# A tile of its own for one set of weight sums, and a new order of adds around two round entries, in a TensorE-bound retention and ELU kernel

## The chip, the cores and the metric

The kernel runs on one core of a Trainium2 chip. The metric is the time of one execution on the device in microseconds (us); lower is better. The kernel computes in float32 (the weights come as float64 bits and are converted at the start).

## The reference, cut to what matters

```
# q, k, v: (4, 8, 768, 64); w_in: (512, 2048); w_out: (2048, 512)
for t in range(S):
    state = gamma * state + einsum('bhd,bhe->bhde', k[:, :, t], v[:, :, t])
    y[:, :, t] = scale * einsum('bhd,bhde->bhe', q[:, :, t], state)
x = y.transpose(0, 2, 1, 3).reshape(3072, 512)
h = x @ w_in
g = where(h > 0, h, exp(minimum(h, 0)) - 1)       # ELU
out = g @ w_out
```

A retention layer with eight heads gives 3072 tokens of 512 values; two matrix products with an ELU between them follow.

## The kernel before, in words

**Tokens.** The 3072 tokens come as six groups of 512 (four chunks of 128 each). Group 0 is multiplied plainly, group 1 with one or two levels of a seven-product scheme, and groups 2 to 5 in two *rounds* of 1024 tokens (`nb` = 0 and 1) with two levels. The retention of a group (`scores`, `states`, `outputs`, cut into `retention_step`s) is laid between the products of an earlier stage. A chunk of q, k and v (1 MB) is loaded into one of four rotating buffers of the pool `ldpool`, tag `chunk` (`load`, L113), and POOL scales its v (`scale_v`, L293).

**The seven products.** A product of 2x2 blocks is made of seven block products instead of eight: inputs are combined by four subtractions beforehand (`quarters_of`, L892), weights by four sums S1 to S4, and the results are put together by adds. The outer products are called M1 to M7 (`j` in the code), the inner ones 1 to 7 (`k`). The results of the outer level are the four blocks C11, C12, C21 and C22.

**The first matrix in a round.** M2, M3, M1 and M7 are made of inner products in eight *steps* (`ORDER1`, `at` = 0 to 7, two halves of each: M2 in steps 0 and 1, M3 in 2 and 3, M1 in 4 and 5, M7 in 6 and 7). `big_twice` (matmuls at L1150) emits a step in pieces: product 1; products 2, 6, 7; product 5; product 4; product 3. ACT lifts results out of PSUM (L1161), DVE adds the others (`plus(r, t)`, L1165: `plus(0,0)` after product 2, `plus(1,1)` after 5, `plus(1,0)` after 4). The loop interleaves two steps, so that PE runs: product 1 of a step, 4 of the step before, 2, 6, 7 of this one, 3 of the one before, 5 of this one. PSUM has a bank `b` and a bank `d`, and two banks `a`. Product 7 of a step uses bank `d`, which `plus(1,0)` of the step before frees.

M1 is kept in two chunk buffers (`held_x`). M2 lands in C11's place, and `big_c11(r, at)` (L1218, one 128x1024 add) adds M1 to a quarter of it. M6, M4 and M5 are not kept: in the *tile loop* (n = 0 to 7, a tile of 128 features each) they are accumulated by `rest(m, j)` (L1197) onto a PSUM bank that ACT filled with M1's tile (`seed`, L1650) and, for M4, onto bank `d`, filled with what the first bank then holds (`second_seed`, L1654, on DVE for odd m and on ACT for even m). `sum_` (L1206) adds the kept results to C21, C12 and C22. The inputs of M6, M5 and M4 are three 128x1024 subtractions of `big_layer_x` (L1118) at the end of its generator: `t1` in step 6, `t2` in step 7 and `t4` behind the steps. An ELU of a tile has two ACTIVATEs on ACT (`begin`, L1212 and L1213, into one of three buffers `r`) and one DVE instruction (`end`, L1214).

**The second matrix** (`second_big`, matmuls at L1246) starts with four quarter inputs of C11 (`input_parts`, L892, 128x1024 each), which the tile loop advances by `next(sec)`.

**Sums of weights in round 0.** For M2, M3, M1 and M7, `combine_small(j)` makes S1 to S4 (four 128x512 DVE instructions, L850), and six stores send them to a scratch in DRAM (`send_small`, L664; for M7 by `sent(7)` in step 3). From there the weights come back piece by piece (L830) into a ring of eight buffers `wq`: `done` gives a buffer free and fetches the next piece on the list, and pieces of M1 and M7 are `blocked` until they are sent. M1's and M7's sums use the same tile, the one of C22 (`gq["C22"]`, shown as gC in the profile). Other stores (`stores`) send the plain weights of M2, M3, M1, M7 and of the layers for round 1.

**What sets the order.** The schedule is by hand: every engine runs its instructions in the order in which the code emits them, and waits for semaphores where data or a buffer isn't ready. All DMAs are issued by SP in one queue. `some(steps, n)`, `run(steps)` and `next(...)` advance the generators; `small_at` and `parts_of` say which step emits what of the weights' sums and of the inputs.

Of the kernel before, what the change touches and what calls it, by code (L numbers as in the profile page):

```python
# [10 lines left out]
FP32 = mybir.dt.float32  # L11
# [8 lines left out]
def kernel(  # L20
# [33 lines left out]
    nc = tc.nc  # L54
    PSUM = bass.MemoryType.PSUM
    P = nc.NUM_PARTITIONS
# [19 lines left out]
    ldpool = ctx.enter_context(tc.tile_pool(name="ldpool", bufs=4))  # L76
# [247 lines left out]
    def scores(tb, pp):  # L324

        sc = [ps_r.tile([P, 2, HP, D], FP32, name="sc", tag="r") for _ in range(2)]
        for x in range(2):
            score_products(sc, tb, pp, x)
        for a in range(2):
            nc.vector.tensor_tensor(  # L330
                out=raw[tb * CPB + 2 * pp + a][0][:, 1].rearrange("p h c -> p (h c)").rearrange("p (n t) -> p n t", t=D),
                in0=sc[a].rearrange("p x h t -> p (x h) t"),
                in1=cmask.unsqueeze(1).to_broadcast([P, 2 * HP, D]), op=ALU.mult,
            )
# [371 lines left out]
    def bank(x):  # L706
        return ps_f.tile([P, 2, TH], FP32, name="p" + x, tag=x, bufs=2 if x == "a" else 1)
# [133 lines left out]

    def combine_small(j):

        if j in (1, 7):
            t = gq["C22"].rearrange("p a t -> p (a t)").rearrange("p (k m c) -> p k m c", k=4, m=4)
        else:
            t = stage.tile([P, 4, 4, P], FP32, name="wi", tag="stage")
        a11, a12, a21, a22 = (W_IN[j][:, 2 * r : 2 * r + 2, :, c, :] for r in range(2) for c in range(2))
        s1, s2, s3, s4 = (t[:, k].rearrange("p (n f) c -> p n f c", f=2) for k in range(4))
        tt = lambda o, x, y, op: nc.vector.tensor_tensor(out=o, in0=x, in1=y, op=op)  # L850
        tt(s1, a21, a22, ALU.add)
        yield
        tt(s2, s1, a11, ALU.subtract)
        yield
        tt(s3, a11, a21, ALU.subtract)
        yield
        tt(s4, a12, s2, ALU.subtract)
        for at in range(2):
            to = scratch3[AMONG[j], at]
            mine = t[:, :, 2 * at : 2 * at + 2].rearrange("p k f d -> p k (f d)")  # L860
            to_send.append((to[1].rearrange("p (k c) -> p k c", k=2), mine[:, 1:3]))
            to_send.append((to[2][:, 0:256], mine[:, 0]))
            to_send.append((to[3][:, 0:256], mine[:, 3]))
# [239 lines left out]
    def big_x(j):  # L1103

        x, t, first_k = xb2 if j == 3 else xa, next_ts(), 0 if j == 1 else 2
        yield from inner_x(j, t, *(x[:, first_k + k, TH * u : TH * u + TH] for k in range(2) for u in range(2)))
# [97 lines left out]
    def big_sum(x, m, ps):  # L1204

        nc.vector.tensor_tensor(out=tile_of(x, m), in0=ps, in1=tile_of("C22" if x == "C21" else x, m), op=ALU.add)  # L1206
# [9 lines left out]
    def big_c11(r, at):  # L1216
        g = G["C11"][r][:, at]
        nc.vector.tensor_tensor(out=g, in0=g, in1=G["M1"][r][:, at], op=ALU.add)  # L1218
# [234 lines left out]
    def run(steps):  # L1453
        for _ in steps:
            pass
# [8 lines left out]
    def some(steps, count):  # L1464
        for _ in itertools.islice(steps, count):
            pass
# [75 lines left out]
    def retention_step(tb, step):  # L1542
        if step == 0:
            scores(tb, 0)
            scores(tb, 1)
        elif step == 1:
            states(tb, 0)
            states(tb, 1)
        else:
            outputs_step(tb, step - 2)  # L1550
# [57 lines left out]
    sec = second_twice(1, lambda: run(big_x(2)))  # L1608
# [11 lines left out]
    for s in sec:  # L1620
        if s == "first":
            step += 1
        at = (step, s if s in ("first", "middle") else "end")
# [16 lines left out]
    for nb in range(NB):  # L1640
        more = nb + 1 < NB
        qa, qd, ends = {}, {}, {}
# [8 lines left out]

        def second_seed(m):
            qd[m] = bank("d")
            (nc.vector.tensor_copy if m % 2 else nc.scalar.copy)(qd[m], qa[m])  # L1654

        def sum_(x, m):
            big_sum(x, m, qd[m] if x == "C21" else qa[m])

        def begin(x, *ms):
            for m in ms:  # L1660
                ends[x, m] = big_elu(x, m)

        def end(x, *ms):
            for m in ms:
                ends.pop((x, m))()
# [5 lines left out]
        def sent(j):  # L1671
            send_small()
            blocked.discard((2, "t", j))
            fetch()
# [9 lines left out]
        def side(at, place):  # L1684
            if nb == 0 and at in small_at and small_at[at][place]:
                j, n = small_at[at][place]
                some(smalls[j], n)
                if n == 3:
                    sent(j)
            if at in parts_of:  # L1690
                some(xparts, parts_of[at][place])
# [6 lines left out]
        for at, (j, sub) in enumerate(ORDER1):  # L1698
            if at == 4:
                held_x = [ldpool.tile([P, 2048], FP32, name="chunk", tag="chunk") for _ in range(2)]  # L1700
                G["M1"] = [x.rearrange("p (n f t c) -> p n f t c", n=2, f=2, t=2) for x in held_x]
            cur = big_twice(nb, j, sub)
            next(cur)
            if at in (6, 7):
                begin("C11", {6: 0, 7: 4}[at])
            if at:
                next(tail, None)
            else:
                run(tail)
            if at in (6, 7):  # L1710
                big_c11(1, at - 6)
            if at == 7:
                end("C11", 0, 1)
            side(at, 0)
            if at == 1 and nb == 0:
                retention_step(3, 2)
            next(cur)
            side(at, 1)
            if nb == 0:
                if at == 0:  # L1720
                    scores(3, 1)
                elif at == 1:
                    retention_step(3, 3)
            run(tail)
            if at == 7:
                seed(0)
            next(cur)
            tail = cur
            if at in (5, 6):
                big_c11(0, at - 5)  # L1730
            if at in (6, 7):
                begin("C11", {6: 1, 7: 5}[at])
            if at == 7:
                end("C11", 4)
            if nb == 0:
                if at == 0:
                    retention_step(3, 1)
                elif at == 1:
                    retention_step(3, 4)
                    run(tail)  # L1740
            side(at, 2)
            if nb == 0:
                if at in (4, 5):
                    bring(groups[0], at - 4)
                stores[at]()
                send_small()
        sec = second_big(nb, (lambda: run(big_x(2))) if more else lambda: None)
        LAST = 2 * NQ - 1
        next(tail)
        rest(0, 6)  # L1750
        second_seed(0)
        some(xparts, 1)
        run(tail)
        seed(1)
# [2 lines left out]
        for n in range(2 * NQ):  # L1757

            if n == 0:
                rest(0, 4)  # L1760
                sum_("C21", 0)
            if n < LAST:
                rest(n + 1, 6)
            if n == LAST - 1 and nb == 0:
                ts_slots[2:2] = [
                    w_all[:, 2 * k : 2 * k + 2, 3072:3584].rearrange("p n (f t) -> p n f t", f=2) for k in range(2)
                ]
            if n:
                begin("C12", n - 1)
            late = {1: 6, 3: 7}.get(n)  # L1770
            if late:
                end("C11", late)
            if n + 2 <= LAST:
                seed(n + 2)
            if n:
                begin("C22", n - 1)
                end("C21", n - 1)
                end("C12", n - 1)
            else:
                begin("C11", 3)  # L1780
                end("C11", 2)
            if n:
                rest(n, 4)
                sum_("C21", n)
            if n < LAST:
                second_seed(n + 1)
            begin("C21", n)
            if n:
                end("C22", n - 1)
            else:  # L1790
                end("C11", 3)
            if n in (0, 2):
                begin("C11", 6 + n // 2)
            if more and n in (1, 5):
                bring(groups[0], 2 + n // 4)
            if n >= LAST - 1:
                next(sec)
                next(sec)
            rest(n, 5)
            sum_("C12", n)  # L1800
            sum_("C22", n)
        next(sec)
        begin("C12", LAST)
        next(sec)
# [10 lines left out]
        for s in sec:  # L1815
# [3 lines left out]
            at = (step, s if s in ("first", "middle") else "end")  # L1819
            if more and at in VISITS:  # L1820
                n = VISITS.index(at)
# [60 lines left out]
```

## Time and profile before

| | |
|---|---|
| runs | 631.17, 630.06, 629.51 us; median 630.06 |
| profiled execution | 631.84 us, of which the span from first to last instruction is 630.0; mean granted TensorE clock 0.991 |
| instructions | 13421 |
| L1150 | x4 (one product of a step): 1.03 us, the next one starts 0.86 to 0.87 later |
| L1197 | x4: 1.88 us, the next one starts 1.72 later |
| L1165, L1206, L1214, L850 (128x512 on DVE) | 0.68 us, the next one starts 0.60 later |
| L1218, L1118, L892 in `second_big` (128x1024 on DVE) | 1.21 to 1.22 us |
| L1161, L1650, L1654 on ACT | 0.57 to 0.59 us |
| DMA | 125.13 MB, mean 199 GB/s |

Of the span, round 0's eight steps take from about 239 to 303 us and its tile loop to 346 us; its second matrix follows, and then round 1 in the same form, with its tile loop from 501 to 541 us. The profile divides the span into 40 slices of 15.75 us; a digit is the busy share of a slice in tenths. An "idle" time stands with the releaser, the instruction or DMA whose end ended the wait; where several semaphores are waited for, the last one by the profile is named.

### The profile page before, as it was taken

What the parts mean: (1) busy time and instruction counts of PE and PEld (TensorE: products, weight loads), DVE (VectorE), ACT (ScalarE), POOL (GpSimd) and SP (SyncE); (2) the same over time, 40 slices, a digit from 0 to 9 for tenths busy, and PEclk for the clock granted to TensorE, in tenths of its full rate; (3) what the DMA queues carried; (4) which work ended last, traced back from release to release, by engine and by line L of the source; (5) the groups of instructions that cost most, each with busy time, mean ns of one, the idle gap of its engine ahead of it and who ended that gap; (6) DMA issues with size and microseconds to landing.
All of it is one profiled execution on the core that took longest, in us unless ns stands there. A gap on an engine that the chain in (4) does not pass through costs nothing.

```text
span 630.0 us, 13421 instructions
## 1 busy us (share of the span) xinstructions
PE 615.2 (98%) x5446; PEld 482.9 (77%) x5446; DVE 498.0 (79%) x778; ACT 259.8 (41%) x444; POOL 25.5 (4%) x30
## 2 busy tenths in 40 slices
PE   7999999999999999979999999999999999999997
PEld 5764568888888998868544888888888744688886
DVE  5769789989788885557888987898546888888885
ACT  5789735114541112225796411010134799511110
POOL 1012000000000110001000000030000000000000
PEclk8999999999999999979999999999999999999999
DMA  8697569699474995398921345774544523355552
GB/s 305 267 380 307 175 205 270 203 269 288 176 237 128 366 389 176 117 281 257 297 68 67 102 129 153 262 278 119 200 152 143 158 68 93 106 152 184 153 152 113
DMA packets 79277, 125.13 MB, mean 199 GB/s; under 512 B 6128, under 2 KB 46832, under 8 KB 74480
## 3 DMA queue, kind: packets, MB, share of 16 engines
q1 hardware_dynamic: 79216, 124.28, 60.7%
q8 instruction: 43, 0.70, 0.4%
q14 instruction: 18, 0.15, 0.1%
HBM read 94.63 MB, written 29.62 MB: 197 GB/s over the span
## 4 chain that ended last, share of the span: by engine, by line
PE 82%; DMA 10%; DVE 4%; SPq 2%; issue 1%; ACT 0%; DVEq 0%
PE pa L1246 16%; PE pd L1246 7%; PE pa L1150 7%; PE pa L1197 5%; PE pb L1246 4%; DMA wq<-scratch_dram 4%; PE pd L1197 4%; PE pa L542 3%; PE x L632 3%; PE pd L1150 3%; PE pa L765 3%; DMA scratch_dram<-w_all 3%; DMA chunk<-in_qkv_dram 2%; PE pa L632 2%; PE pb L1197 2%; PE y L415 2%
## 5 line engine op out<-in xcount | busy, mean ns | idle before, releaser
L1254 ACT COPY ms<-pa 128x256 f32<-128x256 f32 x41 | 15.2, 370 | 104.0 <-PE pa L1246 101.0
L1246 PE MATMUL pa<-gC,wq 128*128 128x256 f32 x224 | 53.4, 383 | 1.0 <-DVE w_all L1206 1.0
L1246 PEld LDWEIGHTS pa<-gC,wq 128*128 128x128 f32 x224 | 41.8, 190 | 8.9 <-DVE w_all L1206 2.6
L1213 ACT ACTIVATE r<-r 128x512 f32<-128x512 f32 x64 | 40.3, 630 | 2.0
L293 POOL TENSOR_TENSOR chunk<-chunk,vf 128x512 f32<-128x512 f32 x16 | 22.7, 1420 | 384.3 <-DMA chunk<-in_qkv_dram 248.7
L1161 ACT COPY m<-pa 128x512 f32<-128x512 f32 x32 | 18.7, 585 | 46.5 <-PE pa L1150 46.4
L1258 DVE TENSOR_TENSOR res<-pd,ms 128x256 f32<-128x256 f32 x26 | 10.9, 421 | 24.3 <-PE pd L1246 14.2
L1150 PE MATMUL pa<-ts,wq 128*128 128x256 f32 x104 | 27.8, 394 | 0.0
L1246 PE MATMUL pa<-ts,wq 128*128 128x256 f32 x112 | 26.9, 383 | 0.0
L1246 PE MATMUL pd<-w_all,wq 128*128 128x256 f32 x112 | 26.5, 379 | 0.0
L171 ACT ACTIVATE w_all<-wraw 128x1024 uint32<-128x1024 uint32 (+1 forms) x19 | 19.2, 1010 | 15.2 <-PE x L632 5.0
L1246 PE MATMUL pd<-ts,wq 128*128 128x256 f32 x104 | 24.6, 379 | 0.0
L1246 PEld LDWEIGHTS pd<-w_all,wq 128*128 128x128 f32 x112 | 21.3, 190 | 2.9
L1150 PEld LDWEIGHTS pa<-ts,wq 128*128 128x128 f32 x104 | 19.9, 195 | 4.7 <-ACT m L1161 0.8
L1246 PEld LDWEIGHTS pa<-ts,wq 128*128 128x128 f32 x112 | 20.9, 190 | 3.3 <-ACT ms L1254 0.3
L1214 DVE SCALAR_TENSOR_TENSOR w_all<-r,w_all 128x512 f32<-128x512 f32 x32 | 21.8, 682 | 1.9 <-ACT r L1213 1.9
L1228 DVE TENSOR_TENSOR gC<-w_all,gC 128x1024 f32<-128x1024 f32 x20 | 23.4, 1216 | 0.0
L1246 PE MATMUL pa<-w_all,wq 128*128 128x256 f32 x96 | 22.9, 381 | 0.0
L173 ACT ACTIVATE w_all<-wraw 128x1024 fp8e4<-128x1024 f32 (+1 forms) x19 | 22.6, 1191 | 0.6
L1197 PE MATMUL pa<-gC,w_all 128*128 128x512 f32 x48 | 22.1, 594 | 0.0
L1197 PE MATMUL pa<-ts,wq 128*128 128x512 f32 x48 | 22.1, 592 | 0.0
L1246 PEld LDWEIGHTS pd<-ts,wq 128*128 128x128 f32 x104 | 19.8, 190 | 2.7
(324 smaller groups left out, 1462.5 us busy)
## 6 DMA issues: line engine op xcount, KB each, us to landing
wq<-scratch_dram SPq DMA_DIRECT2D x191, 256.0 KB, 3.2
chunk<-in_qkv_dram SPq DMA_DIRECT2D x22, 1024.0 KB, 7.3
wraw<-in_w_dram SPq DMA_DIRECT2D x15, 1024.0 KB, 6.0
out_dram<-res SPq DMA_DIRECT2D x7, 512.0 KB, 3.0
scratch_dram<-gT SPq DMA_DIRECT2D x12, 256.0 KB, 4.4
wq<-scratch_dram SPq DMA_DIRECT2D x24, 128.0 KB, 3.2
scratch_dram<-w_all SPq DMA_DIRECT2D x24, 128.0 KB, 4.0
scratch_dram<-w_all SPq DMA_DIRECT2D x12, 256.0 KB, 5.9
```

The source lines that it names most:

```text
L171: nc.scalar.activation(flat, lo, AF.Copy, scale=2.0**-29)
L173: nc.scalar.activation(top, hi.bitcast(FP32), AF.Copy, scale=2.0**-120, saturate=False)
L293: eng.tensor_tensor(out=v, in0=v, in1=vf[:, i].unsqueeze(2).to_broadcast([C, H, D]), op=ALU.mult)
L542: nc.tensor.matmul(hp, lhsT=w[n][:, fi, j // 2, j % 2, :], rhs=xb[:, j, :], start=(j == 0), stop=(j == 3))
L632: nc.tensor.matmul(X[j][:, d, :], lhsT=w[j][:, d * P : d * P + P], rhs=x[j], start=(n == 0 and d == 0), stop=at_end, skip_group_check=True,)
L765: nc.tensor.matmul(ps[:, fi, :], lhsT=w[:, fi, j2, :], rhs=x[:, j2, :], start=(begin and fi == 0 and j2 == 0), stop=(j2 == 1), skip_group_ ...
L1150: nc.tensor.matmul(ps[:, f, :], lhsT=w[:, f, :], rhs=big_xs[j][k], start=(begin and f == 0), stop=True, skip_group_check=True,)
L1197: nc.tensor.matmul(ps, lhsT=w[:, k, :], rhs=layer_x[j][:, k], start=False, stop=(k == 1), skip_group_check=True,)
L1213: nc.scalar.activation(r, r, AF.Exp, scale=-1.0)
L1214: return lambda: nc.vector.scalar_tensor_tensor(g, r, -1.0, g, ALU.add, ALU.max)
L1228: nc.vector.tensor_tensor(out=quarter(to, r, t), in0=quarter(x, r, t), in1=quarter(y, r, t), op=op)
L1246: nc.tensor.matmul(ps, lhsT=w[:, f, :], rhs=ts[j][k][:, f // 2, f % 2, :], start=(begin and f == 0), stop=(f == 3), skip_group_check=True,)
```

## The change

In `combine_small`, M7's sums get a chunk buffer of `ldpool` instead of C22's tile (M1's stay there). `second_seed(7)` moves from DVE to ACT. The four `big_c11` and the ELU ends of C11's tiles 0, 1 and 4 are emitted at other places of steps 6 and 7 and of the tile loop: `big_c11(0, 1)` from the end of step 6 to the end of step 7; `big_c11(1, 1)` from step 7 into the tile loop's n = 0; the end of tile 0 to the end of step 6, of tile 1 to the middle of step 7, of tile 4 behind the second seed of tile 0. In the tile loop's n = 6, two quarter inputs of the second matrix are emitted behind tile 6's last two sums instead of ahead of them.

```
--- before.py
+++ after.py
@@ -841,7 +841,9 @@
 
     def combine_small(j):
 
-        if j in (1, 7):
+        if j == 7:
+            t = ldpool.tile([P, 2048], FP32, name="chunk", tag="chunk").rearrange("p (k m c) -> p k m c", k=4, m=4)
+        elif j == 1:
             t = gq["C22"].rearrange("p a t -> p (a t)").rearrange("p (k m c) -> p k m c", k=4, m=4)
         else:
             t = stage.tile([P, 4, 4, P], FP32, name="wi", tag="stage")
@@ -1651,7 +1653,7 @@
 
         def second_seed(m):
             qd[m] = bank("d")
-            (nc.vector.tensor_copy if m % 2 else nc.scalar.copy)(qd[m], qa[m])
+            (nc.vector.tensor_copy if m in (1, 3, 5) else nc.scalar.copy)(qd[m], qa[m])
 
         def sum_(x, m):
             big_sum(x, m, qd[m] if x == "C21" else qa[m])
@@ -1707,15 +1709,15 @@
                 next(tail, None)
             else:
                 run(tail)
-            if at in (6, 7):
-                big_c11(1, at - 6)
-            if at == 7:
-                end("C11", 0, 1)
+            if at == 6:
+                big_c11(1, 0)
             side(at, 0)
             if at == 1 and nb == 0:
                 retention_step(3, 2)
             next(cur)
             side(at, 1)
+            if at == 7:
+                end("C11", 1)
             if nb == 0:
                 if at == 0:
                     scores(3, 1)
@@ -1726,12 +1728,12 @@
                 seed(0)
             next(cur)
             tail = cur
-            if at in (5, 6):
-                big_c11(0, at - 5)
+            if at in (5, 7):
+                big_c11(0, at // 7)
+            if at == 6:
+                end("C11", 0)
             if at in (6, 7):
                 begin("C11", {6: 1, 7: 5}[at])
-            if at == 7:
-                end("C11", 4)
             if nb == 0:
                 if at == 0:
                     retention_step(3, 1)
@@ -1749,6 +1751,7 @@
         next(tail)
         rest(0, 6)
         second_seed(0)
+        end("C11", 4)
         some(xparts, 1)
         run(tail)
         seed(1)
@@ -1759,6 +1762,7 @@
             if n == 0:
                 rest(0, 4)
                 sum_("C21", 0)
+                big_c11(1, 1)
             if n < LAST:
                 rest(n + 1, 6)
             if n == LAST - 1 and nb == 0:
@@ -1793,12 +1797,15 @@
                 begin("C11", 6 + n // 2)
             if more and n in (1, 5):
                 bring(groups[0], 2 + n // 4)
-            if n >= LAST - 1:
+            if n == LAST:
                 next(sec)
                 next(sec)
             rest(n, 5)
             sum_("C12", n)
             sum_("C22", n)
+            if n == LAST - 1:
+                next(sec)
+                next(sec)
         next(sec)
         begin("C12", LAST)
         next(sec)
```

More of the change, by code (lines that the diff above doesn't have):

```diff
@@ L842, in combine_small @@
     def combine_small(j):
-        if j in (1, 7):
+        if j == 7:
+            t = ldpool.tile([P, 2048], FP32, name="chunk", tag="chunk").rearrange("p (k m c) -> p k m c", k=4, m=4)
+        elif j == 1:
             t = gq["C22"].rearrange("p a t -> p (a t)").rearrange("p (k m c) -> p k m c", k=4, m=4)
@@ L1653, in second_seed @@
             qd[m] = bank("d")
-            (nc.vector.tensor_copy if m % 2 else nc.scalar.copy)(qd[m], qa[m])
+            (nc.vector.tensor_copy if m in (1, 3, 5) else nc.scalar.copy)(qd[m], qa[m])
         def sum_(x, m):
@@ L1709 @@
                 run(tail)
[L1710 to L1713, printed above, removed]
+            if at == 6:
+                big_c11(1, 0)
             side(at, 0)
@@ L1718 @@
             side(at, 1)
+            if at == 7:
+                end("C11", 1)
             if nb == 0:
@@ L1728 @@
             tail = cur
-            if at in (5, 6):
-                big_c11(0, at - 5)
+            if at in (5, 7):
+                big_c11(0, at // 7)
+            if at == 6:
+                end("C11", 0)
             if at in (6, 7):
                 begin("C11", {6: 1, 7: 5}[at])
-            if at == 7:
-                end("C11", 4)
             if nb == 0:
@@ L1751 @@
         second_seed(0)
+        end("C11", 4)
         some(xparts, 1)
@@ L1761 @@
                 sum_("C21", 0)
+                big_c11(1, 1)
             if n < LAST:
@@ L1795 @@
                 bring(groups[0], 2 + n // 4)
-            if n >= LAST - 1:
+            if n == LAST:
                 next(sec)
@@ L1801 @@
             sum_("C22", n)
+            if n == LAST - 1:
+                next(sec)
+                next(sec)
         next(sec)
```

## The prediction, made before the changed kernel ran

> **What bounds the kernel now.** I read the page first. TensorE is busy nearly all the time, so an edit can only win where PE is idle or where its clock is low.
>
> ```profile
> PE 615.2 (98%) x5446; PEld 482.9 (77%) x5446; DVE 498.0 (79%) x778; ACT 259.8 (41%) x444; POOL 25.5 (4%) x30
> ...
> PE   7999999999999999979999999999999999999997
> ...
> PEclk8999999999999999979999999999999999999999
> ```
>
> The one slice inside the kernel where both PE and its clock drop is the eighteenth, 267.75 to 283.5 us. The list of PE's waits names that place first, and then two others that the change touches.
>
> ```profile
> PE pd L1150 <- DVE gT L1165: 4.0, 1, 4.0
> ...
> PE pa L1246 <- DVE w_all L1206: 1.0, 2, 0.5
> PE pd L1197 <- ACT w_all L1161: 0.7, 1, 0.7
> ```
>
> The timeline around 270 us (start, length, engine, line; idle time and its releaser in brackets) shows who is late.
>
> ```profile
> 263.60 0.68 DVE L1165 TENSOR_TENSOR gC<-pb,m 128x512 f32<-128x512 f32 x1
> ...
> 267.24 1.03 PE L1150 MATMUL pa<-ts,wq 128*128 128x256 f32 x4
> ...
> 269.43 0.69 DVE L850 TENSOR_TENSOR gC<-w_all 128x512 f32<-128x512 f32 x1 [5.15 <-DMA scratch_dram<-gC]
> ...
> 271.24 0.42 DVE L892 TENSOR_TENSOR ts<-xt 128x256 f32<-128x256 f32 x1
> 271.57 0.68 DVE L1165 TENSOR_TENSOR gT<-pd,m 128x512 f32<-128x512 f32 x1
> ...
> 272.31 2.08 PE L1150 MATMUL pd<-ts,wq 128*128 128x256 f32 x4 [4.04 <-DVE gT L1165]
> ```
>
> DVE's first sum of M7's weights (L850) overwrites C22's tile, from which M1's sums are still being stored; it waits 5.15 us. DVE works in order, so step 2's `plus(1,0)` at 271.57, which frees bank d, waits behind it, and PE's product 7 of step 3 waits for that. The windows (length, then busy us and count of PE, PEld, DVE, ACT, POOL, then the granted clock) show the second half of the price.
>
> ```profile
> 267.60:271.00 3.40, 0.67 (x4) 0.24 (x2) 1.57 (x3) 0.58 (x1) 0.00 (x0) 1.00 0.76 188
> 271.00:274.40 3.40, 2.09 (x5) 1.74 (x6) 3.40 (x8) 0.00 (x0) 0.00 (x0) 0.50 0.91 262
> 274.40:277.80 3.40, 3.40 (x9) 2.69 (x9) 0.32 (x1) 1.17 (x2) 0.00 (x0) 0.50 1.06 351
> 277.80:281.20 3.40, 3.40 (x17) 2.99 (x17) 2.58 (x4) 0.59 (x1) 0.00 (x0) 0.99 0.94 274
> ```
>
> After a stretch with 0.67 us of work in 3.4, the clock is 0.50 for 6.8 us: 9 matmuls in the third row, 17 in the fourth.
>
> **Part 1, the chunk tile: -6.86 us.** Four sums and six stores stay as they are; only the tile differs. The new tile takes the buffer of group 3's first chunk, whose last reader, PE's L430, ended at 258.3, so the sum has nothing to wait for. DVE's row (a 128x512 follows the one before after 0.60 us) becomes: first sum 264.2, `plus(1,1)` 264.8 (its product ends 264.74), second sum 265.4, input 266.0, `plus(1,0)` 266.6 (its product ends 266.55) to 267.3. Product 7 follows product 6 after one group of 0.865 us, at 268.10, not 272.31: 4.21 us. From there to step 5's product 1 at 283.76 lie ten groups; at full clock, as from 283.76 to 289.89 (seven groups in 6.13), they take 8.80 us, not 11.45: 2.65 us.
>
> By the Trainium skill (TensorE: Matmul & The Clock Gate, What's actually happening) the clock halves after an idle window of about 3.4 us, and the window runs freely. The trace agrees on the length (two such windows at 0.50); what free-running means here is the second rival.
>
> What is late next? Every weight that PE needs 6.86 us sooner comes through SP, whose row doesn't get sooner: from 263.1 to 281.6 SP issues back to back, delayed by earlier transfers and not by DVE (M7's stores go at 273.8 with SP free only at 273.54). I set each fetch's landing in the trace against the new need. Product 6 of step 4 needs its weight at 273.4 (landed 270.8), product 5 of step 5 at 282.2 (279.6), product 6 of step 6 at 285.7 (280.9). The tight one is product 5 of step 7: need 294.2, landed 295.28, behind a 1 MB chunk load. In the trace SP lost 1.4 us before that load waiting for PE to free slots; these waits go, but the DMA engines are 0.9 busy there, so I let the landing come about 1.1 us sooner. I take +0.1; the bounds are 0 and +1.1 (no sooner at all). The new load of a chunk into M7's buffer stands at 293.4; the stores out of it landed by 279.1.
>
> **Part 2, the entry of the rounds: +0.9 us.** PE's first L1197 on pd needs `t4` (DVE L1118, the last quarter input). In round 0 `t4` ended at 306.55 and PE started at 306.70 (the list above says ACT; the DVE row is the one whose end PE's semaphore follows in the trace, as also in round 1). Round 1, DVE's row:
>
> ```profile
> 496.33 1.22 DVE L1118 TENSOR_TENSOR ts<-xb,ts 128x1024 f32<-128x1024 f32 x1
> 497.47 0.68 DVE L1165 TENSOR_TENSOR w_all<-pb,m 128x512 f32<-128x512 f32 x1
> 498.07 0.68 DVE L1165 TENSOR_TENSOR w_all<-pa,m 128x512 f32<-128x512 f32 x1
> 498.67 0.68 DVE L1214 SCALAR_TENSOR_TENSOR gC<-r,gC 128x512 f32<-128x512 f32 x1
> 499.27 0.68 DVE L1165 TENSOR_TENSOR w_all<-pd,m 128x512 f32<-128x512 f32 x1
> 499.87 1.21 DVE L1118 TENSOR_TENSOR w_all<-xt,ts 128x1024 f32<-128x1024 f32 x1
> ```
>
> The row is full up to `t4`; PE loses 0.07 us. The change takes one 128x1024 add (1.13 us to the next) out of it altogether, but puts the other, `big_c11(0,1)`, behind `plus(1,1)` of step 7. That one can't start before its product ends (started 496.64, 1.12 us to DVE, as in step 6: 490.52 to 491.65), at 497.76; DVE idles before it. Then the add 498.36, `plus(1,0)` 499.49, the ELU end 500.09, `t4` 500.69 to 501.90, 0.82 later than 501.08. I take **+0.8**.
>
> Round 0 by the same chain: product 5 starts 301.26 (old time base), `plus(1,1)` 302.38, `t4` 305.31 to 306.52, against 306.55: nothing, since round 0 was as late before for another reason:
>
> ```profile
> 300.57 1.37 POOL L293 TENSOR_TENSOR chunk<-chunk,vf 128x512 f32<-128x512 f32 x1 [5.95 <-DMA chunk<-in_qkv_dram]
> ...
> 300.96 2.06 DVE L1118 TENSOR_TENSOR gC<-xb,gC 128x1024 f32<-128x1024 f32 x1
> ```
>
> An add beside a POOL multiply took 2.06, not 1.22. The multiply follows a chunk's landing (300.50), which comes only some 1.1 us sooner; seen from PE, now 6.86 ahead, it falls on the end of `t4`. I take +0.1, bounds 0 and +0.85.
>
> By the Trainium skill (GPSIMD Engine Reference, 1. Specifications) POOL shares SBUF interfaces with DVE, contending with DVE instructions of two SBUF inputs. `t4` is one, so a full overlap would give the upper bound; these two rows agree.
>
> The add that leaves, `big_c11(1,1)`, now stands behind tile 0's first sum: 1.13 us on DVE, ahead of bank d's second seed. In round 0 that seed moves from 310.41 to about 310.9; PE wants it at 313.6. Hidden; without that cover it would cost 1.1. The ELU ends change order among themselves at 0.60 each, and each buffer of `r` is free before its next use.
>
> **Part 3, tile 6 of the loop: -0.9 us.** In both rounds PE waits 0.48 at L1246 for tile 6's last sum, which frees bank a; two quarter inputs stood ahead of it (343.24 and 344.49, sum at 346.23). Now the sum ends at 344.3, and PE goes on at 346.33. The next gate is ACT's copy of the first product, behind an ELU that waits for DVE's sum of tile 7. One 0.60 us copy has left DVE (the second seed of tile 7, on an ACT that idled 0.96 there), so that comes at 350.1 instead of 350.55: **0.45 a round**, bounds 0 and 0.5.
>
> **The sum.** -6.86 + 0.1 + 0.1 + 0.8 - 0.9 = -6.76. The profiled execution took 631.84 (span 630.0), so its like becomes 625.1. The three runs' median is 630.06, 1.8 lower; I take the same difference from it: **623.3**.
>
> **Rivals.**
> 1. *The weights become the bound.* With DMA 0.9 busy, the weight of step 7 lands no sooner, and a stall there delays later steps: +1 to +3, so 624.3 to 626.3. For it: the full DMA rows. Against: 2 us or more of slack on all other fetches. 0.09.
> 2. *The clock saving is not in the ordinary runs.* If the stretch that decides the clock lies otherwise against 4.04 us of idle time, the clock may not fall; then only 4.21 goes: 630.06 - 4.11 = 626.0. For it: the profiled run is 1.8 above the median. Against: in the windows above idle time was followed by half clock at once. The free-running window of the page named in part 1 is this rival's reason. 0.11.
> 3. *The change doesn't do what it says*: DVE's wait was for something else, or the chunk buffer has a reader that I overlook; parts 2 and 3 cancel, 630.1. Against: the store of M1 is the row's releaser. 0.03.
> 4. *Slower*: one mechanism, at the two round entries. The add now in front of `t4` holds PE; if the hold reaches a stretch like the one at 267.6 to 271.0, the clock halves too, and each entry costs about 4.2 + 2.65, both 13.7; with part 1 and part 3 kept, 13.7 - 6.86 + 0.1 - 0.9 = +6.0 gives 636.1. It decides from some 3.4 us of hold on; I work out 0.8. Slower at all would need the holds to pass 7.7 together. 0.04.
> 5. *The entry costs nothing* and all else holds: 622.4. 0.04.
>
> My forecast has 0.69. The range reaches down to rival 5 with the weights and the second round's ends at their best, 621.6, and up past rival 2 with the bounds of the entry, 626.8. What a measurement of this kernel can tell from no change is about 0.3%, 1.9 us: faster 0.93 (forecast and rivals 1, 2, 5), same 0.03 (rival 3), slower 0.04 (rival 4).
>
> **What would show it.** Right: DVE's L850 beside `chunk` without idle time at about 264; PE's 4.0 gone from its waits; PEclk at 9 in that slice; about 0.8 of PE idle at L1197 in round 1; L1246's two waits gone. Wrong: PE waiting for wq near 294, or an L850 that still waits for a DMA. If the clock row already differs between runs, my median is off by up to 2.65.

## The result, and the profile after

The changed kernel takes **624.83 us** (median of 7 runs, 623.48 to 628.01), the kernel before 630.06 in the same session (7 runs, 626.76 to 631.17). The ratio, which compares means, is 0.9932, 95% interval 0.9904 to 0.9961: faster by less than 1%, with an interval that excludes no change. The median is 1.5 us above the forecast of 623.3, inside its range. The profiled execution is the slowest of the seven, 628.01 (span 626.2). In the changed kernel the lines named here have numbers higher by two (L850 is L852, L1150 is L1152, L1197 is L1199, L1246 is L1248).

The page: PE's row and its clock, which had dropped in the eighteenth slice, are at 9 there now, as in every slice from the third to the last but one.

```profile
PE 612.4 (98%) x5446; PEld 481.7 (77%) x5446; DVE 495.3 (79%) x776; ACT 260.9 (42%) x446; POOL 24.9 (4%) x30
...
PE   7899999999999999999999999999999999999998
...
PEclk8999999999999999999999999999999999999999
```

The timeline around the old stall: the chunk tile's first sum (266.86) follows its neighbour without idle time, and step 2's `plus(1,0)`, which frees bank d, comes at 269.25. PE's product 7 starts at 270.77, straight after product 6.

```profile
266.26 0.69 DVE L1167 TENSOR_TENSOR gC<-pb,m 128x512 f32<-128x512 f32 x1
266.86 0.68 DVE L852 TENSOR_TENSOR chunk<-w_all 128x512 f32<-128x512 f32 x1
...
269.25 0.69 DVE L1167 TENSOR_TENSOR gT<-pd,m 128x512 f32<-128x512 f32 x1
...
269.91 1.03 PE L1152 MATMUL pa<-ts,wq 128*128 128x256 f32 x4
270.77 1.03 PE L1152 MATMUL pd<-ts,wq 128*128 128x256 f32 x4
```

The windows there: PE is busy throughout, at a clock of 1.00 where it was 0.50.

```profile
267.40:270.80 3.40, 3.40 (x18) 2.99 (x17) 3.33 (x7) 0.58 (x1) 0.00 (x0) 1.00 0.69 230
270.80:274.20 3.40, 3.40 (x17) 2.85 (x16) 2.17 (x5) 1.76 (x3) 0.00 (x0) 1.00 0.85 218
```

The list of PE's waits has lost the 4.0 us and holds four that matter: product 5 of step 7 (0.7, new), the two round entries (1.0 and 0.9, before 0.7 and 0.07), and tile 6 (0.6 for both rounds, now named after ACT, before 1.0 after DVE).

```profile
PE pd L1199 <- DVE ts L1120: 1.0, 1, 1.0
PE pd L1199 <- ACT w_all L1163: 0.9, 1, 0.9
...
PE pa L1152 <- ACT w_all L1163: 0.7, 1, 0.7
PE pa L1248 <- ACT ms L1256: 0.6, 2, 0.3
```

**Where the time went.** A median can't part terms of 0.5 us. PE does the same matmuls in the same order in every kernel here, so I took the start of each matmul in one trace minus its start in the trace of before. This difference moves only where PE gains or loses time, and its steps are the terms of the sum. "From" and "to" are times in the kernel before.

```
step of the difference, us          forecast   changed kernel
the tile       (266.6 to 284.7)      -6.86      -6.95
the weight     (300.6 to 302.4)      +0.1       +0.92
entry, round 0 (302.4 to 308)        +0.1        0.00   (-0.25, then +0.25)
tail,  round 0 (308 to 354)          -0.45      -0.46
entry, round 1 (500.3 to 503.8)      +0.8       +0.85
tail,  round 1 (503.8 to 548)        -0.45      -0.46
sum                                  -6.76      -6.09   (all steps after 266.6)
```

Ahead of all this the changed kernel's profiled run is 2.67 us later than before's at 240.7, ahead of the first instruction that the change touches: 1.0 by about 30 us, and 1.7 in group 1's second matrix, where PE waits for `wq` for 1.3 us in all, before 0.2. The edit has no part in this. It is the size of what one run differs from the next, and the reason why the profiled run alone (628.01 against 631.84) shows only 3.83 less.

The weight's place in the timeline: PE waits 0.68 us ahead of product 5 of step 7.

```profile
297.19 0.58 ACT L1163 COPY w_all<-pa 128x512 f32<-128x512 f32 x1 [0.28 <-PE pa L1152]
...
297.83 1.10 PE L1152 MATMUL pa<-ts,wq 128*128 128x256 f32 x4 [0.68 <-ACT w_all L1163]
```

The bracket names ACT's copy, which ended at 297.77. But the matmul reads the slot that a fetch fills, and in the trace that fetch landed at 297.69: the two are within 0.08 us. Experiments 6 and 10 part them. (The step is 0.92, not 0.68, because a product that waits for nothing starts 0.17 ahead of the modelled end of the one before, and the first matmul behind the wait took 0.08 more.)

The entry of round 1 on DVE, row for row as forecast: 1.36 us idle until `plus(1,1)`'s product ends, then the add (494.56), the sum, the ELU end, `t4` (496.89), and PE at 498.21 after 0.92 us.

```profile
493.95 0.69 DVE L1167 TENSOR_TENSOR w_all<-pa,m 128x512 f32<-128x512 f32 x1 [1.36 <-PE pa L1152]
494.56 1.22 DVE L1220 TENSOR_TENSOR gC<-gC,chunk 128x1024 f32<-128x1024 f32 x1
495.69 0.68 DVE L1167 TENSOR_TENSOR w_all<-pd,m 128x512 f32<-128x512 f32 x1
496.29 0.68 DVE L1216 SCALAR_TENSOR_TENSOR gC<-r,gC 128x512 f32<-128x512 f32 x1
496.89 1.22 DVE L1120 TENSOR_TENSOR w_all<-xt,ts 128x1024 f32<-128x1024 f32 x1
...
498.21 1.52 PE L1199 MATMUL pd<-w_all,wq 128*128 128x512 f32 x3 [0.92 <-ACT w_all L1163]
```

### The profile page after: what moved, and what is told of

Read it like the earlier page. It is cut to its first block, busy times and chain, and to the rows that moved or that the text cites. A ratio compares the mean times of both kernels' runs of the same rounds, so it can differ in the third digit from the quotient of the medians.

```text
span 626.2 us, 13424 instructions
## 1 busy us (share of the span) xinstructions
PE 612.4 (98%) x5446; PEld 481.7 (77%) x5446; DVE 495.3 (79%) x776; ACT 260.9 (42%) x446; POOL 24.9 (4%) x30
## 4 chain that ended last, share of the span: by engine, by line
PE 86%; DMA 6%; DVE 3%; SPq 1%; issue 1%; ACT 1%; DVEq 0%; ACTq 0%
PE pa L1248 15%; PE pa L1152 9%; PE pd L1248 7%; PE pa L1199 6%; PE pd L1152 4%; PE pd L1199 4%; DMA wq<-scratch_dram 4%; PE pb L1248 4%; PE pa L542 3%; PE x L632 3%; PE pa L765 3%; DMA chunk<-in_qkv_dram 2%; PE pb L1152 2%; PE pa L632 2%; PE pb L1199 2%; PE y L415 2%
## 5 line engine op out<-in xcount | busy, mean ns | idle before, releaser
L1248 PE MATMUL pa<-gC,wq 128*128 128x256 f32 x224 | 53.2, 382 | 0.3 <-ACT ms L1256 0.3
L1248 PEld LDWEIGHTS pa<-gC,wq 128*128 128x128 f32 x224 | 42.0, 190 | 7.5 <-issue 1.0
L1152 PE MATMUL pa<-ts,wq 128*128 128x256 f32 x104 | 27.1, 385 | 0.7 <-ACT w_all L1163 0.7
L1248 PE MATMUL pa<-ts,wq 128*128 128x256 f32 x112 | 26.9, 383 | 0.3 <-ACT ms L1256 0.3
L1248 PE MATMUL pd<-w_all,wq 128*128 128x256 f32 x112 | 26.5, 379 | 0.0
L1248 PE MATMUL pd<-ts,wq 128*128 128x256 f32 x104 | 24.6, 379 | 0.0
L1248 PEld LDWEIGHTS pa<-ts,wq 128*128 128x128 f32 x112 | 20.9, 190 | 3.7 <-ACT ms L1256 0.7
L1248 PEld LDWEIGHTS pd<-w_all,wq 128*128 128x128 f32 x112 | 21.3, 190 | 2.9
L1152 PEld LDWEIGHTS pa<-ts,wq 128*128 128x128 f32 x104 | 19.2, 190 | 5.5 <-ACT w_all L1163 1.1
L1248 PE MATMUL pa<-w_all,wq 128*128 128x256 f32 x96 | 22.9, 381 | 0.0
L1214 ACT ACTIVATE r<-w_all 128x512 f32<-128x512 f32 x32 | 20.0, 624 | 6.2 <-DVE w_all L1208 6.2
L1199 PE MATMUL pa<-gC,w_all 128*128 128x512 f32 x48 | 22.1, 592 | 0.0
L1199 PE MATMUL pa<-ts,wq 128*128 128x512 f32 x48 | 22.1, 592 | 0.0
```

Of the source, the lines that this page charges most:

```text
L1152: nc.tensor.matmul(ps[:, f, :], lhsT=w[:, f, :], rhs=big_xs[j][k], start=(begin and f == 0), stop=True, skip_group_check=True,)
L1199: nc.tensor.matmul(ps, lhsT=w[:, k, :], rhs=layer_x[j][:, k], start=False, stop=(k == 1), skip_group_check=True,)
L1214: nc.scalar.activation(r, g, AF.Relu, scale=-1.0)
L1248: nc.tensor.matmul(ps, lhsT=w[:, f, :], rhs=ts[j][k][:, f // 2, f % 2, :], start=(begin and f == 0), stop=(f == 3), skip_group_check=True,)
```

## The experiments

The theory: the terms of the forecast add up, each at its own place, and +0.92 at the weight is the landing of a fetch. Rivals: the clock's share is not real; the weight's wait comes from the adds or from ACT; the entries' price is POOL's, not the add's. Each kernel was timed beside the kernel before on the same chip (medians of before: 631.33 for experiments 1 to 4, 632.08 for 5, 6, 8 and 9, 631.11 for 7, 10 and 11). The PE steps are read as above.

**1. The tile alone.** Only the change's first hunk:

```
-        if j in (1, 7):
+        if j == 7:
+            t = ldpool.tile([P, 2048], FP32, name="chunk", tag="chunk").rearrange(...)
+        elif j == 1:
```

> Part 1 alone: M7's sums in a chunk tile, everything else as before. My theory: DVE's 5.15 us wait at L850 goes, PE goes on with product 7 of step 3 about 4.2 us sooner, and the clock stays at 1.00 (2.65 us more); product 5 of step 7 then waits for its weight, about +0.7, and the round's entry, where a POOL multiply no longer meets the add in front, gives back about 0.7: -6.8 us in all, and PE's matmuls around 284 us 6.9 us nearer to the start of step 3 than before. Rival: the clock loss is peculiar to the profiled run before; then the median moves by about -4.1 us only, though the profile shows the wait gone. Second rival: the new tile waits too; then 0.

Measured: 624.84 (ratio 0.9894, 0.9871 to 0.9918). PE steps: -6.94 at the tile, 0.00 at the weight, -0.10 at the entry, sum -7.03. The tile's term stands and a part without the clock (-4.2) falls. Two details were missed: I expected the weight to be 0.7 late, and it landed at 293.38 for a need of 293.65; and POOL's multiply was to miss the entry, but met another add ahead of it, which took 1.96 us beside it at 291.00. DVE's row was full from there down to `t4`, so PE's wait of 0.7 at the entry, which was to go, stayed.

**2. The adds and ELU ends alone**: the hunks that move `big_c11` and `end`.

> Part 2 alone: the four adds and the ELU ends of C11 at their new places, C22's tile, the seeds and the quarter inputs as before. My theory: an add between the last products and t4 makes PE's first L1197 on pd in round 1 wait, +0.8 us there, and leaves round 0 where it was (0 to +0.2), so +0.8 to +1.0 us in all. Rival: the add taken out of the row shortens it, and both entries gain what PE waited there, -0.7 us in round 0 and -0.1 in round 1.

Measured: 631.31 (1.0004, 0.9986 to 1.0023). PE steps: +0.85 at the entry of round 1, 0.00 at that of round 0 (-0.25, +0.25), 0.00 at the weight, and +0.26 at the tile, where the same stall was followed by a somewhat longer stretch of half clock; sum +1.12. The price stands at its place; the median, uncertain by 1.2 us, can't show it. The weight has 6.5 us of slack here, so whether the adds make it late is left to experiment 10.

**3. The tail alone**: `second_seed(7)` on ACT and the quarter inputs behind tile 6's sums.

> Part 3 alone: two quarter inputs behind tile 6's sums, and tile 7's second seed on ACT. My theory: L1246's wait of 0.48 us goes in both rounds, and ACT's copy of the first product gives back some 0.03 to 0.25 of the two matmul groups behind it: -0.45 us a round, -0.9 in all. Rival: the wait only moves to the next products, which need the quarter inputs that now come later: 0.

Measured: 629.74 (0.9975, 0.9953 to 0.9997). PE steps: -0.46 in each round and 0 elsewhere. As forecast, the next gate is ACT's copy: L1246 still waits 0.3 a round.

**4. Is the clock's share real? PE kept busy while it waits.** Before's kernel, with 8 matmuls into an unused bank ahead of product 7 (extra work, no other change):

```
+            if k == 7 and begin and n == 0 and (j, at) == (3, 1):
+                filler = ps_r.tile([P, 512], FP32, name="filler", tag="r")
+                for _ in range(8):
+                    nc.tensor.matmul(filler, lhsT=etab[:, 0, 0, 0:P], rhs=etab[:, 0, 0, 0:512], ...)
```

> The kernel before with eight matmuls of 128x512 on constants put in front of product 7 of step 3 in round 0, into a bank that nothing reads: PE works 3.4 us of the 4.04 that it waits there, and DVE waits for the stores as before. My theory: product 7 starts when it did, but the clock stays at 1.00, so the time falls by 2.65 us. Rival (the clock falls only in some runs, or for another reason than PE's idle time): 0 to -1 us in the median, or a clock row that drops all the same.

Measured: 631.18 (0.9994, 0.998 to 1.0009), a miss by my sizing. Each call shows as two matmul instructions, 0.43 us apart, so the row has 16 of them in 7.03 us. They overran the wait and delayed product 7 by 2.66 us, which the kept clock (mean 0.999) paid back: net -0.08 at the tile. At the entry of round 0 PE gained another 0.84 that nobody forecast: the multiply started after `t2` in this run, and `t2` took 1.22 us, not 2.06. The sum is -0.91. A wash at the tile can't decide, so the next kernel has half as many.

**5. Four filler matmuls**, `range(4)` in the same place.

> The kernel before with four matmuls of 128x512 in front of product 7 of step 3 (each takes two passes of 0.43 us, so 3.4 us in all, where eight took 6.9 and held product 7 up by 2.66 us). My theory: product 7 starts when it did, its wait shrinks to some 0.7 us, the clock stays at 1.00, and PE's matmuls around 284 us come 2.65 us sooner than in the profile before; in the median a little less, -1.7 to -2.65 us, since the half clock lasts 3.4 us in some runs of the kernel before and 6.8 in others (mean clocks of 0.997 and 0.994). Rival: the saving comes from the shorter chain of DVE alone and the clock is a by-product: then 0.

Measured: 627.57 (0.9938, 0.9921 to 0.9954), clock 0.999 to 1.0 in all six runs. Its timeline: DVE still waits 4.88 us for the stores, and PE still can't start product 7 before 272.50, but most of its wait is filled. (With the added lines, L1157 is L1150 and L1172 is L1165.)

```profile
268.56 3.60 PE L1146 MATMUL filler<-etab 128*128 128x512 f32 x8
269.62 0.69 DVE L850 TENSOR_TENSOR gC<-w_all 128x512 f32<-128x512 f32 x1 [4.88 <-DMA scratch_dram<-gC]
...
272.50 1.13 PE L1157 MATMUL pd<-ts,wq 128*128 128x256 f32 x4 [0.34 <-DVE gT L1172]
```

The windows there, to be set beside the 0.50 of before:

```profile
271.00:274.40 3.40, 3.06 (x12) 1.89 (x11) 3.40 (x7) 0.59 (x1) 0.00 (x0) 1.00 0.98 252
274.40:277.80 3.40, 3.40 (x17) 2.85 (x16) 2.14 (x5) 1.17 (x2) 0.00 (x0) 1.00 1.07 352
```

With the stall kept and the clock held, PE gains 2.90 at the tile. Of this, 0.27 is a shorter stall: product 7 starts 4.80 us after product 6, before 5.07. From there to step 5's product 1 it is 8.82 us, before 11.45: 2.63 for the clock. In the changed kernel the two stretches are 0.86 and 8.71, so its 6.95 is 4.21 of idle time and 2.74 of clock. PE's sum here is -3.60, since `t2` missed the multiply again (-0.69 at the entry of round 0).

**6. The changed kernel again, unchanged**, beside the variants below.

> The changed kernel itself, on the same chip as the three others, for comparison with them and with its parts. My theory: the sum of what the parts showed by PE's matmuls, -6.9 (tile), +0.9 to +1.1 (adds), -0.9 (tail) and 0 to +0.9 (the weight): -5.9 to -6.9 us against the kernel before. Rival: the parts help each other, and it is more than 7.

Measured: 624.22 (0.9883, 0.9864 to 0.9902). PE steps: -6.94, weight **0**, entry of round 0 **+0.84**, tail -0.46, entry of round 1 +0.85, tail -0.46; sum -6.17. The sum is that of the first profile within 0.1, by another road: here the weight landed 1.66 us ahead of its need, and the chunk with it, so that POOL's multiply fell on `t4`, which ended at 299.20 (the bracket in PE's row names ACT again):

```profile
296.81 1.32 POOL L293 TENSOR_TENSOR chunk<-chunk,vf 128x512 f32<-128x512 f32 x1 [6.53 <-DMA scratch_dram<-w_all]
...
297.14 2.06 DVE L1120 TENSOR_TENSOR ts<-xt,gC 128x1024 f32<-128x1024 f32 x1
...
299.35 1.10 PE L1199 MATMUL pd<-ts,w_all 128*128 128x512 f32 x2 [1.80 <-ACT r L1214]
```

The same timeline, 5 us earlier, tells what the weight's wait was:

```profile
292.22 1.89 PE L1152 MATMUL pa<-ts,wq 128*128 128x256 f32 x8
...
293.28 0.59 ACT L1163 COPY w_all<-pa 128x512 f32<-128x512 f32 x1 [0.28 <-PE pa L1152]
```

The eight matmuls are the group that ACT's copy reads and, from 293.08 on, product 5 of step 7. It starts ahead of the copy and runs beside it. So the copy isn't what product 5 waits for, though the first profile names it; the fetch is.

**7. The chunk load later**: the changed kernel with `bring(groups[0], ...)`, the loads of group 4's first two chunks, issued behind `stores[at](); send_small()` of steps 6 and 7, not in steps 4 and 5, so that the weights' fetches go ahead of the 1 MB load.

> The changed kernel with only the loads of group 4's first two chunks moved behind the stores of steps 6 and 7; the adds stay where the change put them. My theory: the weight of product 5 of step 7 lands in time in every run, and POOL's multiply of the second chunk no longer stands beside t4, which took 2.06 us instead of 1.22 in the last profile of the changed kernel: t4 is back at 1.2 us and PE's wait for it in round 0 at 1.0 us or less, with round 1's unchanged at 0.9; 0.85 to 1.7 us less than the changed kernel where these two struck, nothing where they did not. Rival: t4 was long for another reason, and stays at 2 us in some profiles.

Measured: 624.07 (0.9904, 0.9879 to 0.9929). The weight landed at 288.31, 4.9 us ahead of its need; `t4` of round 0 took 1.22; both unsteady terms are gone (0 at the weight, 0.00 at the entry), and the sum is -6.99. The ratio's interval overlaps that of experiment 6: less than the runs can tell.

**8. The moved add behind `t4`**: the changed kernel with `big_c11(0, 1)` and the ELU end of tile 4 issued after the last quarter input.

```
-            if at in (5, 7):
-                big_c11(0, at // 7)
+            if at == 5:
+                big_c11(0, 0)
...
-        end("C11", 4)
         some(xparts, 1)
+        end("C11", 4)
+        big_c11(0, 1)
```

> The changed kernel with big_c11(0, 1) and the ELU end of tile 4 behind t4. My theory: the add in front of t4 was what PE waited for at the rounds' entries, so PE's first L1197 on pd starts right behind the products: -1.05 us in round 1 and -0.9 in round 0 against the changed kernel, 8 us under the kernel before. Rival: DVE is full there in any order, and the two instructions only push the next ones, the second seed of tile 1 and the first sums: 0.

Measured: 623.03 (0.9865, 0.9833 to 0.9897), its profiled run 620.63. PE steps: entry of round 0 -1.13 (changed kernel 0.00 and +0.84), entry of round 1 -0.25 (changed kernel +0.85); sum -9.18. DVE's row there: `t4` follows the last sum at once; the ELU end and the add now stand behind it. The two moved together (0.60 and 1.13 us of DVE's row), and no run parts them.

```profile
488.42 0.69 DVE L1167 TENSOR_TENSOR w_all<-pd,m 128x512 f32<-128x512 f32 x1
489.02 1.22 DVE L1120 TENSOR_TENSOR w_all<-xt,ts 128x1024 f32<-128x1024 f32 x1
...
490.76 1.22 DVE L1220 TENSOR_TENSOR gC<-gC,chunk 128x1024 f32<-128x1024 f32 x1
```

**9. Both**, the add behind `t4` and the later load.

> As the one before, and the loads of group 4's first two chunks stand behind the stores of steps 6 and 7 instead of ahead of those of steps 4 and 5. My theory: the weight of product 5 of step 7 no longer queues behind 1 MB, so PE's wait there (0.92 us in the profile of the changed kernel) goes, and no POOL multiply falls on DVE's adds in steps 6 and 7: 0.3 to 1.5 us under the one before, as the wait differs between runs. Rival: that wait was ACT's, as the list of waits has it, and stays; and the loads come late for the second matrix, which lays group 4's retention between its products: 0 or slower.

Measured: 623.35 (0.9867, 0.9849 to 0.9885); PE steps as in experiment 8, sum -9.24. The weight is 5 us in time, but it wasn't late in experiment 8 either (0.16 ahead): no gain where there was no wait.

**10. No moved adds**: the tile and the tail, part 2 left out.

> Parts 1 and 3 without part 2: the tile, the seed and the quarter inputs as changed, the adds and the ELU ends of C11 as before. My theory: part 2 is a loss; without it PE waits 0.07 us in round 1's entry and 0.7 in round 0's, so PE's matmuls at the end come 7.9 to 8.1 us sooner, counted from the start of step 3, than in the kernel before (6.1 to 6.2 with part 2). Rival: with the tile's wait gone, the adds in front of step 7 hold the entry back as much: 6.2.

Measured: 624.05 (0.989, 0.9873 to 0.9908). PE steps: -6.94, weight +0.87, entry of round 0 -0.87, tails -0.45 each, entry of round 1 0; sum -7.84. The weight is late here without the moved adds, so part 2 isn't its cause. It cost next to nothing in the end: PE came to the entry later by about as much as it waited there in experiment 1 (0.71). With the first profile there are now two traces with a late weight. From the fetch's landing to the matmul's start they have 0.135 and 0.136 us, from the end of ACT's copy 0.06 and 0.01: the start keeps its distance to the fetch.

**11. Experiment 8 again**, beside experiments 7 and 10.

> Once more the changed kernel with big_c11(0, 1) and the ELU end of tile 4 behind t4, beside the two others on one chip. My theory: 9.2 us by PE's matmuls from step 3 on, 1.2 more than without the adds moved at all, so the lowest of the three in the median by about 1 us, as far as 6 to 12 runs show it. Rival: its 623.0 of the last set, only 1.2 below the changed kernel, was the true gap, since what PE wins is given back before the end: then it ends level with the one without the adds.

Measured: 623.53 (0.9883, 0.9864 to 0.9903); PE sum -8.9, with a step of +0.32 near 429 us, far from the edit. The medians of 7, 10 and 11 lie within 0.6 us though their PE sums lie 1.9 apart: the order of these three rests on PE's steps of one execution each, not on the medians.

## Why the prediction was right, step by step

**The tile, -6.86 forecast.** Eight executions with the chunk tile show -6.94 or -6.95. The split is shown as well: 4.21 of idle time, as forecast, and for the clock 2.74 in the changed kernel's rows and 2.63 with the wait filled (experiment 5), against the 2.65 worked out from ten groups' lengths. The 0.09 that the sum was short is in those lengths: at full clock the ten groups take 8.71, not 8.80.

**Rival 2, the clock saving not in ordinary runs**, holds for some runs, but not for their mean: experiment 1's ratio leaves 5.2 to 8.1 us, more than the idle time's 4.2, and experiment 5, which keeps the stall and holds the clock, saves 2.9 to 5.0. Three profiled executions have the stall unfilled (before, the adds alone, the tail alone), and each has some 6.8 us of half clock behind it. Of the other runs only the mean clock is listed: 6.8 us at 0.50 lose 3.4 of 630, a mean of 0.995, and 3.4 us a mean of 0.997. In the call of experiments 1 to 4 the kernel before stood at 0.993 to 0.995 in 16 of 29 runs (median 631.83), at 0.996 or 0.997 in 12 and at 0.999 in one (the 13: median 630.83); the tile alone stood at 1.000 in five of six. A mean doesn't tell the place, and before's profiled run has another 3.4 us of half clock at 11.6 to 15.0 us (mean 0.991); so in the 12 runs the half clock behind the stall lasted 3.4 us or less, and in the one at 0.999 next to nothing. The Trainium skill (TensorE: Matmul & The Clock Gate, What's actually happening) has an idle window of about 3.4 us that runs freely; mean clocks that differ between runs of one kernel go with this. But the window ahead of the half clock had 0.67 us of work in before's trace, so "idle" isn't "without any work" here. Ahead of the other half clock, from 8.2 to 11.6 us, there were even 1.81 us of work in 3.4. With 3.06, in experiment 5, the clock stayed. It also stayed over 3.4 us with 1.60 of work in experiment 6 (296.4 to 299.8), but that stretch need not be one of the clock's windows. Where the limit lies, no run shows.

**The weight, +0.1 taken, bounds 0 and +1.1.** This is the term that was mis-sized in the profiled run: +0.92. PE waiting for `wq` near 294 was one of the prediction's own signs of being wrong, and it came (at 297 in this run, which is 2.66 us later than before already ahead of the change). What failed is the step "I let the landing come about 1.1 us sooner" as one number. Counted from step 3, the landing came 0.25, 2.6, 1.2, 0.3, 1.1 and 1.45 us sooner in the six executions with the chunk tile and the load at its old place: 1.1 is a fair middle, but it is a lottery of the run, landing against need:

```
              kernel before  changed  again  tile alone  no adds  behind t4  again   late load
landed            295.28     297.69  291.42    293.38    294.20    292.50   295.42    288.31
PE needs it at    301.27     296.99  293.08    293.65    293.54    292.66   295.91    293.24
late by            -5.99      +0.70   -1.66     -0.27     +0.66     -0.16    -0.49     -4.93
```

With the slack down from 6 us to about none, the landing is late in two of six such executions, by 0.7. Moving the chunk load behind the fetches gives 4.9 us of slack, so the 1 MB load ahead of the fetch is the cause, and not ACT's copy, which the profile names (experiments 6 and 10). So rival 1 happened in its mildest form (one fetch, some runs); no other fetch came late in the steps.

**Entry of round 0, +0.1 taken, bounds 0 and +0.85.** 0.00 in the first profile, +0.84 in the second, where POOL's multiply fell on `t4`: exactly the two ends. Which one comes depends on the chunk's landing. Where the multiply started first, an add right behind its start took 2.06 or 1.96 us, against 1.22 without. Where the add started first, the multiply was lengthened instead: in before's trace the add at 292.50 took 1.21 beside a multiply from 292.68 that took 1.94, against 1.04 at its shortest. The Trainium skill (GPSIMD Engine Reference, 1. Specifications), by which POOL and DVE contend where DVE has two SBUF inputs, agrees with these rows; the prediction didn't ask which of the two comes first. In the first profile it was `t4`, from 301.96, and the multiply came at 303.10. That before's entry was late for this reason, as the prediction said, shows in experiments 4 and 5: with `t2` at 1.22, PE was through the entry 0.84 and 0.69 us sooner. Seen over the two profiles the two lotteries are one: an early chunk lets the weight land in time but puts the multiply on `t4` (0 and +0.84), a late one does the opposite (+0.92 and 0). That is why the sums agree, -6.09 and -6.17; with two profiles it is a reading, not a proof. It was luck that no profile of the changed kernel has both: together they would have cost 1.76, where the forecast took 0.2. The later load, which is clear of both, gives -6.99.

**Entry of round 1, +0.8:** +0.85 in all four executions with the add ahead of `t4` (three kernels), 0 without part 2, -0.25 with the add behind. The chain, down to the 1.36 us of idle time ahead of `plus(1,1)`, is that of the forecast. Rival 5 (the entry costs nothing) falls; rival 4 (holds that halve the clock) falls, the holds being 0.96 and 0.92 us, and 1.80 in experiment 6, at full clock. Rival 3 falls with the chunk tile's row in the timeline (266.86).

**The tails, -0.45 each:** -0.45 or -0.46 in every kernel that has them, with ACT's copy the next gate, as forecast. The sign "L1246's two waits gone" was too strong: 0.3 a round is left, now for ACT.

**The median.** Measured are 5.2 us less than before by the medians and 4.3 by the means (by the interval of the ratio 2.5 to 6.0), and 7.9 and 7.4 less in the second timing of the same kernel (6.2 to 8.6). PE's steps give 6.1 and 6.2, between the two. Why the two timings differ isn't settled; the 2.67 us that the first profile lost ahead of the first changed instruction would do for it, if other runs of that session lost as much, which no trace shows. The forecast's 623.3 was 1.5 too low against the first timing: 0.8 of it is the weight's term by the profile, and the rest is within what runs differ by.

**The better version** is the one with the add and the ELU end behind `t4`: 0.9865 and 0.9883 of before, PE sums -9.18 and -8.9, about 3 us below the changed kernel's by PE's steps; by medians 1.2 in the one call that has both, with overlapping intervals. Part 2 as written costs 0.85 at round 1's entry against no part 2 (experiment 10), and gains only once the add no longer stands ahead of the instruction that PE waits for.

## What to carry to other kernels

When an engine that works in order waits for a buffer, look at what is queued behind the wait: here one tile's reuse held a sum that freed a PSUM bank, and the PE stall of 4.0 us cost 6.9, since the clock fell too. Making PE earlier takes slack from every transfer that isn't made earlier with it; a landing whose margin shrinks to nothing should be priced as a chance with both ends, or moved ahead of the large load before it. An add that is merely moved near a stage's entry belongs behind the instruction that the bottleneck engine waits for.

## What the runs showed of the hardware

- Behind one wait of 4 us the clock stood at 0.50 for 6.8 us in each of three profiles, while the mean clock of 12 of 29 runs leaves room for 3.4 at most. Useless matmuls in the wait kept it at 1.00, worth 2.63 us in PE's rows. A window of 3.4 us with 1.81 us of work, at 8.2 us, was followed by half clock too.
- An fp32 matmul of 128x512 ran as two instructions, 0.43 us apart, in the filler rows (16 instructions for 8 calls, 7.03 us).
- The name in a wait's bracket was the wrong one where two releasers ended within 0.08 us of each other (ACT's copy and the fetch); an execution in which the fetch came early told them apart.
- Of a POOL multiply and a DVE add of 128x1024 with two SBUF inputs that overlapped, the one that started second was lengthened: the add to 2.06 (experiment 6, from 297.14), or the multiply to 1.94 (before, from 292.68).
- The landing of one and the same fetch, against its need, varied by 2.4 us between two executions of the same kernel (+0.70 and -1.66).
